# Attention and two feed-forward layers: the weight parts of the third product made beside the second

## The chip, the cores and the metric

The kernel runs on one core of one Trainium2 chip. The metric is the time of one execution on the device in microseconds (us). The kernel before was timed in 3 runs; the median is 1670.05 us.

## The reference

The inputs are q, k, v (batch 8, 8 heads, 576 positions, head size 64) and four weight matrices, all float32. First comes softmax attention inside chunks of 64 positions; its output is laid out as 4608 tokens with 512 features. Then two feed-forward layers follow, each with an inner size of 2048:

```
x = attention(q, k, v)                            # 4608 x 512
x = square(relu(x @ moe_w_in)) @ moe_w_out        # products 1 and 2
h = x @ moe2_w_in                                 # product 3
g = where(h >= 1, h, where(h <= -1, 0, (h + 1)**2 / 4))
out = g @ moe2_w_out                              # product 4
```

The weights come as float64 and are read as pairs of 32-bit words; the kernel decodes them to float32 on the chip.

## The kernel before

**Arithmetic.** Every float32 product is made of three matmuls on parts: an operand is split into hi (rounded) and lo (what is left), and hi x hi, lo x hi and hi x lo are added up. Products 2 to 4 are done in seven block products (P1 to P7) instead of eight, by a scheme of sums of blocks (Strassen and Winograd). So from four blocks of a weight, four sums are made, and the seven block operands that are used are each split into hi and lo.

**Stages.** Four stages follow each other on TensorE (PE). The first makes product 1 block by block of 512 tokens, with the attention of the following tokens beside it. The second (w = 0 in the code) makes product 2, the third product 3, the fourth (w = 1) product 4. Results go through DRAM from stage to stage.

**Order.** The order of the work is written out by hand. Time is counted in slots: one slot is 6 matmuls of a product on PE. `pe_slot` puts matmuls into a slot, `at_slot` the work of the other engines and the DMAs. The program is emitted slot by slot, and each engine works through its own queue strictly in this order, waiting on semaphores. All DMAs are issued by SyncE's queue (SP), so one DMA that waits holds up every later one.

**The first stage** has 288 slots. The attention is done in 72 units of four heads and 128 tokens; from the twelfth on, one unit's turn stands in every four slots (`turn`, PER = 4). A turn loads q and k of the unit four turns on, and every second turn the v of a token tile (`load_v`, 4 DMAs, in slot 4k + 3), which the product with the attention weights (`att_d`, line 367) uses three turns later, in slot 4k + 12. The squares of each product-1 tile are written by GpSimd (line 425) and stored to DRAM (line 431). Besides, 48 weight units are made, one in 5.1 slots: m = 0 for w_out1 (product 2), m = 1 for w_in2 (product 3), m = 2 for w_out2 (product 4), 16 of each. Every unit is loaded by two DMAs (`stage_unit`) and decoded on ACT and DVE (`unit_a`, the first line of `unit_b`). For m = 0 and m = 1 GpSimd then makes the four sums (`sums`, line 184), ACT casts seven blocks to hi (`unit_c`, line 209), DVE subtracts to lo (`unit_d`, line 218), and SP stores hi and lo, 448 KB each (lines 213 and 219). For m = 2 only the four decoded blocks are stored (`wq`, 256 KB, line 201). From slot 192 to 238 SP also loads the first 24 weight tiles of product 2 (`load_w`, line 245). Units of m = 1 stand in slots 103 to 185, those of m = 2 from slot 185 on.

**The second stage** has 280 slots: five pairs of token ranges, each with seven ranks of eight slots, one for each block product. For each two slots `prep_b` puts a split of one operand on ACT (line 443, cast to oh) and DVE (line 444, subtraction to ol) into the program, five slots ahead, into one of three buffer pairs; `comb_b` makes the sums of raw operands on DVE (line 448). `load_g` (line 547) loads the raw operands of the next pair. GpSimd has nothing to do there.

**The third stage** also makes what is left of m = 2: `late_a` loads the four blocks of a unit, `late_b` makes the sums on GpSimd, `late_c` the cast on ACT (line 233), `late_d` the subtraction on GpSimd (line 238) and both stores, at 0, 4, 6 and 7 slots from the unit's start, one unit in ten slots. These four steps share one tile for the blocks and one for hi. The r tiles 10, 11 and 12 (`rt`) hold squares in the first stage and activations in the third; the second stage does not use them.

Of the kernel before, what the change touches and what calls it, by code (L numbers as in the profile page):

```python
# [8 lines left out]
F32 = mybir.dt.float32  # L9
F32R = mybir.dt.float32r  # L10
U32 = mybir.dt.uint32
AF = mybir.ActivationFunctionType
ALU = mybir.AluOpType
AX = mybir.AxisListType

P = 128
# [7 lines left out]

FMAX = 3.4028234663852886e38
RANK = ("P1", "P5", "P6", "P3", "P7", "P2", "P4")
CIDX = {"P4": 0, "P1": 1, "P2": 2, "P5": 3, "P6": 4, "P7": 5, "P3": 6}
SIZES = (448, 448, 448, 480, 480)


# [1 line left out]
def chunk_attention_moe_moe2(ctx, tc, q, k, v, w_in1, w_out1, w_in2, w_out2, out):  # L32
# [10 lines left out]
    nc = tc.nc  # L43
# [9 lines left out]
    HF = NF // 2  # L53
# [10 lines left out]
    mp = ctx.enter_context(tc.tile_pool(name="mp", bufs=1))  # L64
    dram = ctx.enter_context(tc.tile_pool(name="dram", bufs=1, space=bass.MemoryType.DRAM))
# [4 lines left out]
    def f(ap):  # L70
        return ap.bitcast(F32)
# [8 lines left out]
        return pool.tile(shape, dt, tag=f"q{tag}", name=name, padded_shape=[P, 2, n])  # L80

    def rt(tag, shape, name, dt=F32, padded=None):
        return mp.tile(shape, dt, tag=f"r{tag}", name=name, padded_shape=padded or [P, 512])

    def bank(i, shape, name, padded=None):
        return ps.tile(shape, F32, tag=f"b{i}", name=name, padded_shape=padded or [P, 512])
# [10 lines left out]

    wd = {(m, a): dram.tile([P, 2, 2, 7, P], F32, name=f"w{m}_{a}") for m in range(3) for a in range(8)}

    wq = {(a, b): dram.tile([P, 4, P], F32, name=f"q{a}_{b}") for a in range(8) for b in range(2)}  # L100

# [2 lines left out]
    wst = {}  # L106
# [51 lines left out]
    def stage_unit(m, a, b):  # L158
        t = ep.tile([P, 4 * P, 2], U32, tag="ws", name="wu", bufs=2)
        w = (w_out1, w_in2, w_out2)[m]  # L160
        if m == 1:
            src = w.rearrange("(kh kt p) f -> kt p kh f", kh=2, kt=2)[b]
            cols = [(a + fh * HF) * 2 * P for fh in (1, 0)]
        else:
            src = w.rearrange("(kh kk p) d -> kk p kh d", kh=2, kk=HF)[a]
            cols = [(2 * dh + b) * 2 * P for dh in (1, 0)]
        for i, c in enumerate(cols):
            nc.sync.dma_start(
                out=t[:, 2 * i * P:2 * (i + 1) * P].rearrange("p (h f) w -> p h (f w)", h=2),
                in_=src[:, :, c:c + 2 * P],  # L170
            )
        wst[m, a, b] = t
# [7 lines left out]

    def sums(c):

        for o, x, z, op in ((4, 0, 1, ALU.add), (6, 2, 0, ALU.subtract), (5, 4, 2, ALU.subtract), (7, 3, 5, ALU.subtract)):
            nc.gpsimd.tensor_tensor(out=c[:, o], in0=c[:, x], in1=c[:, z], op=op)

    def store_parts(m, a, b, hi, lo):
        nc.sync.dma_start(out=wd[m, a][:, 0, b], in_=f(hi))
        nc.sync.dma_start(out=wd[m, a][:, 1, b], in_=f(lo))

    def unit_b(m, a, b):  # L190
        y, ab = wst[m, a, b]
        if m == 2:
            c = ep.tile([P, 4, P], F32, tag="wl", name="wq", bufs=2, padded_shape=[P, 7, P])
        else:
            c = ep.tile([P, 8, P], F32, tag="wc", name="wc", bufs=1)
        nc.vector.scalar_tensor_tensor(
            out=c[:, 0:4].rearrange("p a f -> p (a f)"), in0=ab, scalar=TINY, in1=f(y), op0=ALU.is_ge, op1=ALU.mult
        )
        wst[m, a, b] = c
        if m == 2:  # L200
            nc.sync.dma_start(out=wq[a, b], in_=c[:, 0:4])
            del wst[m, a, b]
        else:
            sums(c)

    def unit_c(*u):
        c = wst[u]
        hi = ep.tile([P, 7, P], F32R, tag="wh", name="wh", bufs=2)
        nc.scalar.copy(hi, c[:, 1:8])
        wst[u] = (c, hi)  # L210

    def unit_hi(m, a, b):
# [2 lines left out]
    def unit_d(m, a, b):  # L215
        c, hi = wst.pop((m, a, b))
        lo = ep.tile([P, 7, P], F32R, tag="wl", name="wl", bufs=2)
        nc.vector.tensor_tensor(out=lo, in0=c[:, 1:8], in1=f(hi), op=ALU.subtract)
        nc.sync.dma_start(out=wd[m, a][:, 1, b], in_=f(lo))


    def late_a(a, b):
        c = mp.tile([P, 8, P], F32, tag=f"q{LATE[0]}", name="lc")
        nc.sync.dma_start(out=c[:, 0:4], in_=wq[a, b])
        wst[a, b] = c

    def late_b(a, b):
        sums(wst[a, b])

    def late_c(a, b):  # L230
        c = wst[a, b]
        hi = mp.tile([P, 7, P], F32R, tag=f"q{LATE[1]}", name="lh", padded_shape=[P, 8, P])
        nc.scalar.copy(hi, c[:, 1:8])
        wst[a, b] = (c, hi)

    def late_d(a, b):
        c, hi = wst.pop((a, b))
        nc.gpsimd.tensor_tensor(out=c[:, 1:8], in0=c[:, 1:8], in1=f(hi), op=ALU.subtract)
        store_parts(2, a, b, hi, c[:, 1:8])

    wt = {}

# [383 lines left out]
    SB1 = 2 * NF * NBL  # L626
# [9 lines left out]
    LATE = (4, 5)  # L636
# [9 lines left out]
    def at_slot(s, fn, *args):  # L646
        s = int(s)
        assert cur[0] is None or s >= cur[0], (s, cur)
        todo.setdefault(s, []).append((fn, args))
# [4 lines left out]
    with tc.manual_schedule():  # L654
        early = tc.tile_pool(name="early", bufs=1, side="right")
        ep = early.__enter__()
# [93 lines left out]
        for n, u in enumerate(units):  # L750
            g = U0 + n * UPER
            if n < 2:
                at_slot(g - 3 + n, stage_unit, *u)
            at_slot(g, unit_a, *u)
            if n + 2 < len(units):
                at_slot(g, stage_unit, *units[n + 2])
            at_slot(g + 2, unit_b, *u)
            if u[0] < 2:
                at_slot(g + 4, unit_c, *u)
                at_slot(g + 5, unit_hi, *u)  # L760
                at_slot(g + 6, unit_d, *u)
# [44 lines left out]
        for kp in range(4):  # L806
            for n, i in enumerate((0, 1, 3)):
                at_slot(done + 1 + 5 * n + kp, load_g, 0, 0, i, kp)
            at_slot(SB1 + 4, load_g, 0, 0, 2, kp)

        for j in range(NPAIR):
            for i in range(HF):
                b = SA2 + 7 * (HF * j + i)
                for prod, o in OFFS.items():
                    pe_slot(b + o, form_a, j, i, prod)
        for j in range(NPAIR):
            if j == 0:
                e = SA2
                loads = tuple(e - 24 + n for n in range(4))
                times = dict(P1=e - 14, P5=e - 11, P6=e - 8, P3=e - 6, P2=e - 3, P7=e - 2, P4=e + 1)  # L820
            else:
                b = SA2 + 7 * (HF * j - 1)
                l0 = SA2 + 7 * (HF * (j - 1) + 2)
                loads = tuple(l0 + 7 * n for n in (0, 1, 3, 2))
                times = dict(P1=b - 8, P5=b, P6=b + 4, P3=b + 3, P2=b + 5, P7=b + 10, P4=b + 10.5)
            for i in range(4):
                at_slot(loads[i], load_xa, j, i, A_RAW[i])
            for prod in sorted(ORD, key=times.get):
                at_slot(times[prod], prep_a, j, prod)
                if prod in AFTER:  # L830
                    at_slot(times[prod] + (4 if prod == "P2" and j else 1), comb_a, j, prod)
            if j + 1 < NPAIR:
                for n in range(4):
                    g = SA2 + 56 * j + 12 + 10 * n
                    u = divmod(4 * j + n, 2)
                    for d, fn in ((0, late_a), (4, late_b), (6, late_c), (7, late_d)):
                        at_slot(g + d, fn, *u)


        for t in range(56):  # L840
# [63 lines left out]
```

## Time and profile before

| what | us |
|---|---|
| median of 3 runs (1668.27 to 1672.38) | 1670.05 |
| the profiled execution | 1671.81 |
| its span, first to last instruction | 1670.0 |
| first stage ends | 593.5 |
| second stage | 593.5 to 946.6 |
| third stage | 946.6 to 1307.8 |
| fourth stage | 1307.8 to 1662.5 |
| PE / DVE / ACT / GpSimd busy in the span | 1613.6 / 1140.2 / 891.8 / 420.3 |

All times inside the profile are microseconds from the first instruction. Busy time of an engine doesn't count DMA issue, so SP's work is read from its own rows in order of time. A row of waits names the instruction that waited and the one that released it. Loads of matmul weights into PE (PEld) run beside matmuls. PE's granted clock is 0.993 of full speed over the span.

### The profile page before, as it was taken

Reading aid. Unit: us, or ns where it says so; the run is one execution under the profiler, and the core shown is the slowest. Engines: PE = TensorE matmul, PEld = TensorE weight load, DVE = VectorE, ACT = ScalarE, POOL = GpSimd, SP = SyncE. Lnnn points to the kernel's source line nnn. Section 1 sums busy time; section 2 is a strip of 40 time slices with the busy share of each in tenths; the row PEclk is TensorE's granted clock in tenths of the full one; section 3 lists DMA queues with packets and bytes.
Section 4 is the critical chain, followed back from the end, with each engine's and each line's share of the span. In section 5 each row is a group of like instructions: output and inputs, shape, how many; then the busy total and the mean of one; then the engine's idle time right before and its main releaser. Section 6 shows DMA issues by size and latency. Waiting matters only on the chain.

```text
span 1670.0 us, 27722 instructions
## 1 busy us (share of the span) xinstructions
PE 1613.6 (97%) x9504; PEld 1384.6 (83%) x9504; DVE 1140.2 (68%) x1576; ACT 891.8 (53%) x1852; POOL 420.3 (25%) x466
## 2 busy tenths in 40 slices
PE   6889999999999999999999999999999999999998
PEld 4667777777777889999888898988888899998887
DVE  6967666666645267677677757667574778777776
ACT  6656666666555244444444566666665544444442
POOL 2546565556433410000000234344240000000000
PEclk9999999999999999999999999999999999999999
DMA  7667888888888897335277864655659963654723
GB/s 186 185 183 227 266 267 275 263 271 276 254 254 262 265 290 237 98 123 174 72 230 208 247 229 162 240 173 181 227 201 340 306 188 82 161 140 103 200 40 48
DMA packets 445645, 339.51 MB, mean 203 GB/s; under 512 B 217152, under 2 KB 421952, under 8 KB 445504
## 3 DMA queue, kind: packets, MB, share of 16 engines
q1 hardware_dynamic: 445504, 337.74, 67.2%
q8 instruction: 75, 1.23, 0.3%
q14 instruction: 66, 0.54, 0.1%
HBM read 195.04 MB, written 142.61 MB: 202 GB/s over the span
## 4 chain that ended last, share of the span: by engine, by line
PE 79%; DVE 7%; DMA 7%; issue 3%; ACT 2%; POOL 1%; SPq 1%; POOLq 0%; DVEq 0%; ACTq 0%
PE X L454 31%; PE ph L412 19%; PE V L454 17%; PE W L454 7%; DMA vt<-in_v_dram 2%; PE psD L367 2%; DMA wu<-in_moe_w_out_dram 1%; PE psB L311 1%; PE psA L294 1%; DVE wy L115 1%; DMA ws<-in_moe_w_in_dram 1%; DVE ol L444 1%; DVE wy L118 1%; PE psC L352 1%; DVE t L535 1%
## 5 line engine op out<-in xcount | busy, mean ns | idle before, releaser
L454 PE MATMUL X<-oh,w 128*128 128x448 f32 (+1 forms) x1920 | 557.8, 371 | 5.1 <-DVE c L515 5.0
L443 ACT CAST oh<-gr 128x896 fp32r<-128x896 f32 (+1 forms) x280 | 270.0, 964 | 335.0 <-PE X L454 158.1
L444 DVE TENSOR_TENSOR ol<-gr,oh 128x896 fp32r<-128x896 f32 (+1 forms) x280 | 314.4, 1124 | 182.1 <-ACT oh L443 173.4
L454 PEld LDWEIGHTS X<-oh,w 128*128 128x128 f32 x1920 | 360.0, 188 | 48.2 <-ACT t L529 4.3
L454 PE MATMUL X<-ol,w 128*128 128x448 f32 (+1 forms) x960 | 356.7, 372 | 6.4 <-POOL ol L444 5.2
L454 PE MATMUL V<-oh,w 128*128 128x448 f32 (+1 forms) x960 | 278.5, 371 | 0.0
L412 PE MATMUL ph<-xh,ih 128*128 128x512 f32 x576 | 246.5, 428 | 0.2 <-ACT g L424 0.2
L412 PE MATMUL ph<-xl,ih 128*128 128x512 f32 x576 | 228.9, 397 | 0.0
L412 PE MATMUL ph<-xh,il 128*128 128x512 f32 x576 | 228.8, 397 | 0.0
L425 POOL TENSOR_TENSOR g<-g 128x512 f32<-128x512 f32 x144 | 169.6, 1178 | 158.2 <-ACT g L424 148.8
L454 PEld LDWEIGHTS X<-ol,w 128*128 128x128 f32 x960 | 180.1, 188 | 29.7 <-POOL ol L444 6.8
L454 PEld LDWEIGHTS V<-oh,w 128*128 128x128 f32 x960 | 180.2, 188 | 20.9
L448 DVE TENSOR_TENSOR gr<-gr,gr 128x896 f32<-128x896 f32 (+1 forms) x160 | 177.8, 1111 | 3.6 <-DMA gr<-g 3.6
L454 PE MATMUL V<-ol,w 128*128 128x448 f32 (+1 forms) x480 | 178.0, 371 | 0.0
L424 ACT ACTIVATE g<-ph 128x512 f32<-128x512 f32 x144 | 86.5, 601 | 110.7 <-PE ph L412 100.5
L454 PE MATMUL W<-oh,w 128*128 128x448 f32 (+1 forms) x480 | 139.4, 371 | 0.0
L412 PEld LDWEIGHTS ph<-xl,ih 128*128 128x128 f32 x576 | 109.9, 191 | 25.0
L412 PEld LDWEIGHTS ph<-xh,ih 128*128 128x128 f32 x576 | 109.9, 191 | 22.3 <-ACT g L424 0.5
L444 POOL TENSOR_TENSOR ol<-xr,oh 128x896 fp32r<-128x896 f32 (+1 forms) x15 | 36.5, 2434 | 363.2 <-ACT oh L443 352.1
L412 PEld LDWEIGHTS ph<-xh,il 128*128 128x128 f32 x576 | 110.6, 192 | 16.9
L529 ACT ACTIVATE t<-c,half 128x448 f32<-128x448 f32 (+1 forms) x120 | 81.2, 681 | 71.2 <-DVE c L515 71.0
L535 DVE SCALAR_TENSOR_TENSOR t<-c,t 128x448 f32<-128x448 f32 (+1 forms) x120 | 93.1, 802 | 17.6 <-ACT t L529 17.4
(69 smaller groups left out, 2014.2 us busy)
## 6 DMA issues: line engine op xcount, KB each, us to landing
w<-w SPq DMA_DIRECT2D x168, 256.0 KB, 5.2
gr<-g SPq DMA_DIRECT2D x96, 448.0 KB, 5.1
gr<-g SPq DMA_DIRECT2D x64, 480.0 KB, 4.6
g<-t SPq DMA_DIRECT2D x96, 224.0 KB, 2.6
wu<-in_moe_w_out_dram SPq DMA_DIRECT2D x64, 256.0 KB, 4.8
g<-t SPq DMA_DIRECT2D x64, 240.0 KB, 5.0
w<-wh SPq DMA_DIRECT2D x32, 448.0 KB, 3.8
w<-wl SPq DMA_DIRECT2D x32, 448.0 KB, 4.7
```

The source lines that it names most:

```text
L115: nc.vector.scalar_tensor_tensor(out=y, in0=w1, scalar=0xC0000000, in1=y, op0=ALU.bitwise_and, op1=ALU.bitwise_or)
L118: nc.vector.scalar_tensor_tensor(out=y, in0=w0, scalar=29, in1=y, op0=ALU.logical_shift_right, op1=ALU.bitwise_or)
L367: nc.tensor.matmul(pt[rows(e), e, p * P + c * CH:p * P + (c + 1) * CH], vt[u // UT % NV][rows(e), c, u % UT * NP + p, :], at[rows(e), p, r ...
L412: nc.tensor.matmul(ph, win[fi][wi][:, kt * P:(kt + 1) * P], x[:, i, :], start=(kt == 0 and a == 0), stop=(kt == KT - 1 and a == 2),)
L424: nc.scalar.activation(out=g, in_=ph, func=AF.Relu)
L425: nc.gpsimd.tensor_tensor(out=g, in0=g, in1=g, op=ALU.mult)
L443: nc.scalar.copy(hi, raw)
L444: eng.tensor_tensor(out=lo, in0=raw, in1=f(hi), op=ALU.subtract)
L448: eng.tensor_tensor(out=o, in0=x, in1=z, op=ALU.subtract)
L454: nc.tensor.matmul(o, wt_[:, wi, c, :], x[:, i, :], start=first and a == 0, stop=last and a == 2, skip_group_check=True,)
L529: nc.scalar.activation(out=t, in_=h, func=AF.Square, bias=half, scale=0.5)
L535: nc.vector.scalar_tensor_tensor(out=t, in0=h, scalar=1.0, in1=t, op0=ALU.max, op1=ALU.min)
```

## The change

The units of m = 1 get the treatment that those of m = 2 have. In the first stage they are only decoded, and their four blocks are stored in DRAM (`wq`, now also keyed by m). Sums, hi and lo are made in the second stage by the same four `late` steps, in halves of a unit (64 of 128 columns): 32 halves, one in 7.5 slots, from slot 2 of the second stage to slot 241. A half loads 128 KB in pieces of 256 bytes; its two stores write 224 KB each in pieces of 256 bytes. Its tiles are r10 and r12 in turn for the blocks and r11 for hi. The 32 halves are finished before the weights of product 3 are loaded from slot 224 of the stage on, unit by unit.

A unit's tile holds seven blocks instead of eight: one sum is written over a block that no later sum reads, the block pairs are loaded in the other order, and the table CIDX that finds a block product's weights follows. In the third stage the units of m = 2 stay whole and where they were.

```diff
--- before.py
+++ after.py
@@ -24,7 +24,7 @@
 
 FMAX = 3.4028234663852886e38
 RANK = ("P1", "P5", "P6", "P3", "P7", "P2", "P4")
-CIDX = {"P4": 0, "P1": 1, "P2": 2, "P5": 3, "P6": 4, "P7": 5, "P3": 6}
+CIDX = {"P1": 0, "P2": 1, "P7": 2, "P4": 3, "P5": 4, "P6": 5, "P3": 6}
 SIZES = (448, 448, 448, 480, 480)
 
 
@@ -80,7 +80,9 @@
         return pool.tile(shape, dt, tag=f"q{tag}", name=name, padded_shape=[P, 2, n])
 
     def rt(tag, shape, name, dt=F32, padded=None):
-        return mp.tile(shape, dt, tag=f"r{tag}", name=name, padded_shape=padded or [P, 512])
+        if padded is None:
+            padded = [P, 512] if len(shape) == 2 else [P, shape[1], 512 // shape[1]]
+        return mp.tile(shape, dt, tag=f"r{tag}", name=name, padded_shape=padded)
 
     def bank(i, shape, name, padded=None):
         return ps.tile(shape, F32, tag=f"b{i}", name=name, padded_shape=padded or [P, 512])
@@ -97,7 +99,7 @@
 
     wd = {(m, a): dram.tile([P, 2, 2, 7, P], F32, name=f"w{m}_{a}") for m in range(3) for a in range(8)}
 
-    wq = {(a, b): dram.tile([P, 4, P], F32, name=f"q{a}_{b}") for a in range(8) for b in range(2)}
+    wq = {(m, a, b): dram.tile([P, 4, P], F32, name=f"q{m}_{a}_{b}") for m in (1, 2) for a in range(8) for b in range(2)}
 
 
 
@@ -160,10 +162,10 @@
         w = (w_out1, w_in2, w_out2)[m]
         if m == 1:
             src = w.rearrange("(kh kt p) f -> kt p kh f", kh=2, kt=2)[b]
-            cols = [(a + fh * HF) * 2 * P for fh in (1, 0)]
+            cols = [(a + fh * HF) * 2 * P for fh in (0, 1)]
         else:
             src = w.rearrange("(kh kk p) d -> kk p kh d", kh=2, kk=HF)[a]
-            cols = [(2 * dh + b) * 2 * P for dh in (1, 0)]
+            cols = [(2 * dh + b) * 2 * P for dh in (0, 1)]
         for i, c in enumerate(cols):
             nc.sync.dma_start(
                 out=t[:, 2 * i * P:2 * (i + 1) * P].rearrange("p (h f) w -> p h (f w)", h=2),
@@ -180,25 +182,21 @@
 
     def sums(c):
 
-        for o, x, z, op in ((4, 0, 1, ALU.add), (6, 2, 0, ALU.subtract), (5, 4, 2, ALU.subtract), (7, 3, 5, ALU.subtract)):
+        for o, x, z, op in ((4, 2, 3, ALU.add), (2, 0, 2, ALU.subtract), (5, 4, 0, ALU.subtract), (6, 1, 5, ALU.subtract)):
             nc.gpsimd.tensor_tensor(out=c[:, o], in0=c[:, x], in1=c[:, z], op=op)
-
-    def store_parts(m, a, b, hi, lo):
-        nc.sync.dma_start(out=wd[m, a][:, 0, b], in_=f(hi))
-        nc.sync.dma_start(out=wd[m, a][:, 1, b], in_=f(lo))
 
     def unit_b(m, a, b):
         y, ab = wst[m, a, b]
-        if m == 2:
+        if m > 0:
             c = ep.tile([P, 4, P], F32, tag="wl", name="wq", bufs=2, padded_shape=[P, 7, P])
         else:
-            c = ep.tile([P, 8, P], F32, tag="wc", name="wc", bufs=1)
+            c = ep.tile([P, 7, P], F32, tag="wc", name="wc", bufs=1)
         nc.vector.scalar_tensor_tensor(
             out=c[:, 0:4].rearrange("p a f -> p (a f)"), in0=ab, scalar=TINY, in1=f(y), op0=ALU.is_ge, op1=ALU.mult
         )
         wst[m, a, b] = c
-        if m == 2:
-            nc.sync.dma_start(out=wq[a, b], in_=c[:, 0:4])
+        if m > 0:
+            nc.sync.dma_start(out=wq[m, a, b], in_=c[:, 0:4])
             del wst[m, a, b]
         else:
             sums(c)
@@ -206,7 +204,7 @@
     def unit_c(*u):
         c = wst[u]
         hi = ep.tile([P, 7, P], F32R, tag="wh", name="wh", bufs=2)
-        nc.scalar.copy(hi, c[:, 1:8])
+        nc.scalar.copy(hi, c)
         wst[u] = (c, hi)
 
     def unit_hi(m, a, b):
@@ -215,28 +213,40 @@
     def unit_d(m, a, b):
         c, hi = wst.pop((m, a, b))
         lo = ep.tile([P, 7, P], F32R, tag="wl", name="wl", bufs=2)
-        nc.vector.tensor_tensor(out=lo, in0=c[:, 1:8], in1=f(hi), op=ALU.subtract)
+        nc.vector.tensor_tensor(out=lo, in0=c, in1=f(hi), op=ALU.subtract)
         nc.sync.dma_start(out=wd[m, a][:, 1, b], in_=f(lo))
 
 
-    def late_a(a, b):
-        c = mp.tile([P, 8, P], F32, tag=f"q{LATE[0]}", name="lc")
-        nc.sync.dma_start(out=c[:, 0:4], in_=wq[a, b])
-        wst[a, b] = c
-
-    def late_b(a, b):
-        sums(wst[a, b])
-
-    def late_c(a, b):
-        c = wst[a, b]
-        hi = mp.tile([P, 7, P], F32R, tag=f"q{LATE[1]}", name="lh", padded_shape=[P, 8, P])
-        nc.scalar.copy(hi, c[:, 1:8])
-        wst[a, b] = (c, hi)
-
-    def late_d(a, b):
-        c, hi = wst.pop((a, b))
-        nc.gpsimd.tensor_tensor(out=c[:, 1:8], in0=c[:, 1:8], in1=f(hi), op=ALU.subtract)
-        store_parts(2, a, b, hi, c[:, 1:8])
+    n_l = [0]
+
+    def late_a(m, a, b, h):
+        n_l[0] += 1
+        cols = slice(0, P) if m == 2 else slice(h * P // 2, (h + 1) * P // 2)
+        if m == 2:
+            c = mp.tile([P, 7, P], F32, tag=f"q{LATE[0]}", name="lc", padded_shape=[P, 8, P])
+        else:
+            c = rt(10 + 2 * (n_l[0] % 2), [P, 7, P // 2], "lc")
+        nc.sync.dma_start(out=c[:, 0:4], in_=wq[m, a, b][:, :, cols])
+        wst[m, a, b, h] = c, cols
+
+    def late_b(*u):
+        sums(wst[u][0])
+
+    def late_c(*u):
+        c, cols = wst[u]
+        if u[0] == 2:
+            hi = mp.tile([P, 7, P], F32R, tag=f"q{LATE[1]}", name="lh", padded_shape=[P, 8, P])
+        else:
+            hi = rt(11, [P, 7, P // 2], "lh", F32R)
+        nc.scalar.copy(hi, c)
+        wst[u] = (c, cols, hi)
+
+    def late_d(*u):
+        c, cols, hi = wst.pop(u)
+        nc.gpsimd.tensor_tensor(out=c, in0=c, in1=f(hi), op=ALU.subtract)
+        m, a, b, h = u
+        nc.sync.dma_start(out=wd[m, a][:, 0, b, :, cols], in_=f(hi))
+        nc.sync.dma_start(out=wd[m, a][:, 1, b, :, cols], in_=c)
 
     wt = {}
 
@@ -755,7 +765,7 @@
             if n + 2 < len(units):
                 at_slot(g, stage_unit, *units[n + 2])
             at_slot(g + 2, unit_b, *u)
-            if u[0] < 2:
+            if u[0] == 0:
                 at_slot(g + 4, unit_c, *u)
                 at_slot(g + 5, unit_hi, *u)
                 at_slot(g + 6, unit_d, *u)
@@ -807,6 +817,11 @@
             for n, i in enumerate((0, 1, 3)):
                 at_slot(done + 1 + 5 * n + kp, load_g, 0, 0, i, kp)
             at_slot(SB1 + 4, load_g, 0, 0, 2, kp)
+
+        for n in range(32):
+            u = (1, n // 4, n // 2 % 2, n % 2)
+            for d, fn in ((0, late_a), (4, late_b), (6, late_c), (7, late_d)):
+                at_slot(SB1 + 2 + 7.5 * n + d, fn, *u)
 
         for j in range(NPAIR):
             for i in range(HF):
@@ -834,7 +849,7 @@
                     g = SA2 + 56 * j + 12 + 10 * n
                     u = divmod(4 * j + n, 2)
                     for d, fn in ((0, late_a), (4, late_b), (6, late_c), (7, late_d)):
-                        at_slot(g + d, fn, *u)
+                        at_slot(g + d, fn, 2, *u, 0)
 
 
         for t in range(56):
```

## Rows read from the trace of the kernel before

**Rows 1.** busy us (count): PE, PEld, DVE, ACT, POOL; clock, DMA, GB/s
```profile
258.40:414.40 156.00, 151.88 (x1281) 120.73 (x1279) 105.90 (x200) 101.53 (x315) 92.93 (x125) 0.98 0.87 268
414.40:565.00 150.60, 144.59 (x1103) 115.14 (x1100) 80.27 (x165) 78.46 (x254) 60.95 (x61) 1.00 0.87 256
...
593.50:946.60 353.10, 352.22 (x1681) 315.08 (x1681) 258.95 (x254) 156.90 (x183) 6.82 (x4) 1.00 0.60 182
```

**Rows 2.** what PE waited for, 258.4 to 565: total us, times, longest
```profile
PE psD L367 <- DMA vt<-in_v_dram: 7.6, 9, 2.5
PE psD L367 <- ACT wa L111: 1.5, 1, 1.5
```

**Rows 3.** chain that ended last: start, us, what
```profile
349.36 2.95 PE ph L412 x12
356.60 2.95 PE ph L412 x12
```

**Rows 4.** by stretch, of line 412 alone: PE busy (count), PEld busy (count)
```profile
46.10:318.20 272.10, 217.77 (x811) 148.63 (x811) 0.97 0.79 237
...
258.37:412.03 153.66, 127.92 (x481) 87.52 (x481) 0.98 0.87 268
412.03:530.10 118.07, 94.11 (x361) 64.26 (x362) 1.00 0.88 257
```

**Rows 5.** SP's queue in order of time, 330 to 344: start, us, what
```profile
329.63 0.42 SPq L431 DMA_DIRECT2D g<-g  x1
330.14 0.40 SPq L213 DMA_DIRECT2D w<-wh  x1
330.65 1.56 SPq L168 DMA_DIRECT2D wu<-in_moe_w_in_dram  x2
332.30 0.99 SPq L431 DMA_DIRECT2D g<-g  x2
333.41 3.29 SPq L283 DMA_DIRECT2D vt<-in_v_dram  x4
```

**Rows 6.** PE in order of time, 338 to 340 [idle before <- releaser]
```profile
339.09 1.05 PE L367 MATMUL psD<-atT,vt 64*64 64x64 f32 x12 [2.48 <-DMA vt<-in_v_dram]
```

**Rows 7.** instructions of the tiles wl and wq: ns min/median/max, first and last start
```profile
L218 DVE TENSOR_TENSOR wl<-wc,wh x32: 1075/1092/1931, 122.8 to 420.2; 128x896 fp32r<-128x896 f32 x32
L219 SPq DMA_DIRECT2D w<-wl x32: 338/457/1136, 124.0 to 429.8; - x32
...
  DVE wq L196: 5.8, 2
...
L201 SPq DMA_DIRECT2D q<-wq x16: 364/402/1124, 433.2 to 563.8; - x16
```

**Rows 8.** what SP's queue waited for, 258.4 to 414.4
```profile
SPq L431 <- POOL wc L184: 3.8, 9, 0.8
```

**Rows 9.** DVE in order of time, 660 to 675
```profile
668.29 1.09 DVE L444 TENSOR_TENSOR ol<-gr,oh 128x896 fp32r<-128x896 f32 x1 [0.26 <-ACT oh L443]
```

**Rows 10.** PE in order of time, 668 to 673
```profile
672.59 0.37 PE L454 MATMUL V<-ol,w 128*128 128x448 f32 x1
```

**Rows 11.** by tile: qkn (258 to 565), lc, gr and w (593 to 946)
```profile
DMA to landing us min/median/max: 2.3/3.0/4.2
...
L184 POOL TENSOR_TENSOR lc<-lc x64: 452/462/932, 963.3 to 1220.6; 128x128 f32<-128x128 f32 x64
...
L233 ACT CAST lh<-lc x16: 927/944/947, 968.2 to 1221.5; 128x896 fp32r<-128x896 f32 x16
L238 POOL TENSOR_TENSOR lc<-lc,lh x16: 2127/2134/2335, 969.2 to 1222.5; 128x896 f32<-128x896 f32 x16
...
DMA to landing us min/median/max: 3.4/5.1/7.0
...
L245 SPq DMA_DIRECT2D w<-w x78: 517/571/1787, 596.6 to 944.7; - x78
```

**Rows 12.** what ACT waited for, 946 to 1308
```profile
ACT lh L233 <- POOL lc L184: 3.5, 4, 1.6
```

## Prediction

> **What bounds the kernel now.** I read the stages first, as stretches of time: the first product with the attention beside it ends at 593.5 us, the second product (w = 0) runs to 946.6, the third to 1307.8, the fourth to the end. In the second product TensorE is busy 352.22 of 353.10 us, GpSimd 6.82 and DVE 258.95 [rows 1]: that stage has no time to give, only time to lose. In the two stretches of the first stage in which the units of w_in2 (m = 1, 258.4 to 414.4) and of w_out2 (m = 2, 414.4 to 565.0) are made, TensorE is short of its stretch by 4.1 and 6.0 us, and the DMA engines stand at 0.87 [rows 1].
>
> Next, what TensorE waits for there: the load of v, 7.6 us in 9 waits of 10.1 in all; nothing else is above 1.5 [rows 2]. TensorE's own beat says how much is lost with all that follows a wait: an undisturbed turn (four slots, 24 matmuls, and one attention unit) is 356.60 - 349.36 = 7.24 us [rows 3]. 480 matmuls (20 turns; one more is counted at the edge) took 153.66 us where 144.8 would do, so 8.9 us were lost; the next 360 (15 turns) took 118.07 instead of 108.6, 9.5 lost [rows 4]. That is 18.4 us in the stretch that the change touches.
>
> Then why v is late. SyncE's queue (SP) issues every DMA of the kernel, in program order. By 318.2 TensorE has started the 810 matmuls of slots 0 to 134 (and one more at the edge) [rows 4]. Slot 135 is where the program puts the load of the token tile that slot 144 uses. SP issues it at 333.41, 15.2 us after TensorE came to slot 135; TensorE stands 2.48 us and begins with that v at 339.09 [rows 5, 6]. SP does not idle before this: its rows follow each other with gaps of 0.09 to 0.12 us [rows 5]. So SP is a second full engine in this stage. It lags TensorE by two turns, and whenever the lag and the landing together pass the 16.3 us of the nine slots from 135 to 144 (9 x 7.24/4), TensorE pays.
>
> **The change part by part.**
> *First stage, taken out.* Each of 16 units of m = 1 loses its four sums on GpSimd, the cast on ACT, the subtraction on DVE, and the stores of hi and lo (448 KB each); it gets one store of the decoded blocks (256 KB). For SP that is one DMA less for a unit: 0.46 us of issue (the w<-wl median; the new store is like q<-wq, 0.40 [rows 7]) and 0.10 of gap, 16 x 0.56 = 9.0 us. SP also waited 3.8 us in this stretch for g behind GpSimd's sums [rows 8]; those sums go. SP's relief is thus 9.0 to 12.8 us. DVE, ACT and GpSimd each lose work too, but TensorE's waits there are for v, so I count that at nothing beyond the 3.8. The stalls of m = 1 go first; what SP has left over it carries into the stretch of m = 2, where 24 loads of w are squeezed in and the lag would otherwise build up again. As long as SP is the late queue, a microsecond that it saves is one that TensorE saves. Bounds for this step: 18.4 (no stall left) and 4 (what TensorE stands idle in the stretch of m = 1, with those of m = 2 as before). I take 10, a little over the issues alone. SP's lag at the loads of w is what is late next.
>
> *First stage, moved.* The border between units with hi and lo and units with a store of blocks comes 16 units earlier. The blocks' tile shares two buffers with lo, and DVE waited 5.8 us in two waits for the stores of lo at the old border [rows 7]. Behind it in DVE's queue stand the row maxima of the attention, on which the exponentials wait. At the old border TensorE shows no wait for DVE [rows 2]; at the new one SP lags about as much. Between 0 and 5.8 I take +0.5, near the old border's price on TensorE.
>
> *Second product, added.* 32 half units, one in 7.5 slots, which are 7.5 x 353.1/280 = 9.46 us: SP a load of 128 KB in 256-byte pieces and two stores of 224 KB in 256-byte pieces; GpSimd four sums of 64 columns and a subtraction of 448; ACT a cast of 448. What can reach TensorE:
> (a) ACT's queue. The cast waits for the sums, the sums for the load, and behind the cast stand the splits of the operands. The split of the second rank's first operand starts at 668.29, takes 1.09 and is first read at 672.59 [rows 9, 10]: 3.2 us ahead. So TensorE does not see an ACT delay up to some 3 us.
> (b) Whether that wait comes. Program order makes the half units serial: SP's store of n stands ahead of the load of n + 1. The loop is load 3.0 (the nearest row: q and k, up to 128 KB in 256-byte pieces) + four sums of 0.37 (between half of 0.462 and the whole) + cast 0.5 (half of 0.944, with a start) + subtraction 1.1 (half of 2.134) + issue of the second store 0.9 (over the 0.571 of w<-w in 512 pieces; here 896) + six semaphore steps of 0.1 = 7.6 us [rows 11]. That is under 9.46: ACT finds the sums ready. In the third product the same loop on whole units let ACT wait 3.5 us in all [rows 12]. At the far end (load 4.2, sums 0.93) it is 11.0, at the near end (2.3 and 0.23) 6.3.
> (c) SP itself: 96 issues of 0.6 to 0.9 us in 300. The raw loads for the next pair stand 11 slots and more ahead of their use, against a landing of 5.1 [rows 11].
> The first half unit's buffer holds one of the last g of the first stage, so SP holds the loads of w for some 3 us; these are wanted 30 slots later. For all this +1.0, between 0 and the price of rival 2.
>
> *Third product.* A unit's tile has seven blocks instead of eight, in another order; the same counts and sizes of operations: 0.
>
> Sum: -10 + 0.5 + 1.0 = -8.5. The profiled execution took 1671.8 us (span 1670.0), 1.8 over the median of the runs: 1663.3 by it, 1661.5 against the median of 1670.05.
>
> **The rivals.**
> 1. *SP's relief is used up* in the stretch of m = 2: the loads of w bring the lag back to its limit, and only m = 1's 4 us go. For it: 9.5 us are lost there although its units have three DMAs already. Against it: SP would start that stretch with less lag. -4 + 1.5 = -2.5: 1667.5.
> 2. *The loop in the second product outlasts its 7.5 slots* (slower than before). If the small loads land like gr (5.1) and the sums take 0.46, it is 5.1 + 1.84 + 0.5 + 1.1 + 0.9 + 0.6 = 10.0 us, 0.58 over; 32 x 0.58, less the cover of 3.2, is 15.4 us of TensorE, paid at the cast in ACT's queue. It outweighs the 9.5 of the first stage from a loop of 9.46 + 12.7/32 = 9.86. Net +5.9: 1676. For it: the DMA share of 0.60 goes up [rows 1]. Against it: q and k landed in 3.0 at a share of 0.87.
> 3. *GpSimd blocks DVE.* A subtraction of 896 columns on DVE took 1.08 at best and up to 1.93 in the first stage, where GpSimd works beside it [rows 7]. A half unit brings 2.6 us of GpSimd. Taken as a full block, DVE's demand in 303 us (240 slots) is 222 + 32 x 2.6 = 305: over the brim, and in the two ranks of each pair in which DVE both combines and evicts the cover of 3.2 goes. I price 0.8 us in each of these ten, 8 us: net -1.5, 1668.5. At half a block DVE has 264 of 303 and nothing is lost, which is what I take.
> The Trainium skill, SBUF — State Buffer (Who interferes with whom), says that a DVE instruction with two SBUF inputs contends with a GpSimd one that reads SBUF, and that whichever comes second waits for the whole of the other. By that rule rival 3 is the forecast. The spread from 1.075 to 1.931 agrees that they collide; the median of 1.092 doesn't show that most overlaps cost their whole length.
> 4. *All stalls go*: -18.4 + 1.5 = -16.9, 1653.
>
> **How the numbers follow.** Forecast 0.57 (own range 1657 to 1666), rival 1 0.18, rival 2 0.10, rival 3 0.10, rival 4 0.05. Less than 0.3% (5.0 us) can't be told from no change. Faster: 0.51 of the forecast, 0.04 of rival 1, 0.02 of rival 3, 0.05 of rival 4: 0.62. Same: 0.06 + 0.13 + 0.06 + 0.01 of rival 2 = 0.26. Slower: 0.09 of rival 2, 0.02 of rival 3, 0.01 of rival 1: 0.12. The range, 1654 to 1672, leaves out rival 2, most of rival 4 and the tails.
>
> **What would show it.** Right: the lag of SP behind slot 135 falls under 12 us, TensorE's waits for v shrink below 5 us, the first stage ends near 584, the second product lasts 353 to 355. Wrong: v is late by the same amount with SP idle before it (then the transfer, not the queue, is the limit); ACT's lh waits for lc by more than 20 us in the second product, with TensorE waiting for ol (rival 2); DVE's splits there at 1.4 and over with TensorE waiting (rival 3).

## Result: slower by 1%, and the profile after

The changed kernel takes 1686.74 us (median of 4 runs, 1684.11 to 1688.01); the kernel before took 1670.76 beside it. The ratio is 1.0095, 95% interval 1.0076 to 1.0113. Forecast were 1661.5 and a range up to 1672: the first stage gained about what was forecast, and the second lost twice as much.

| stage (us of the profiled run) | before | after | |
|---|---|---|---|
| first stage ends | 593.5 | 580.3 | -13.2 |
| second stage | 353.1 | 380.2 | +27.1 |
| third stage | 361.2 | 362.6 | +1.4 |
| fourth stage | 354.7 | 355.1 | +0.4 |
| span | 1670.0 | 1685.8 | +15.8 |

**First stage.** Matmuls of product 1 by stretch, slots 0 to 134, 104 to 183 and 184 to 243 (PE busy with count, PEld busy with count, clock, DMA share, GB/s); the counterparts are [rows 4]:

```profile
45.60:314.90 269.30, 217.45 (x811) 148.69 (x811) 0.97 0.78 234
...
255.40:403.50 148.10, 126.91 (x480) 86.74 (x481) 0.99 0.79 230
403.50:517.00 113.50, 94.97 (x360) 64.89 (x361) 0.98 0.82 238
```

480 matmuls take 148.10 us, 3.3 above the undisturbed 144.8; the next 360 take 113.50, 4.9 above 108.6. So 8.2 us are lost where 18.4 were. This profile and those of eight runs below have the same first stage; they lose 4.5 to 8.2 us in these slots and end the stage between 577.4 and 583.1 us. So the gain there is 10 to 14 us, and a difference of some 4 us between two such profiles shows nothing by itself. TensorE comes to slot 135 at 314.9 and SP issues that slot's load of v 9.2 us later, against 15.2 [rows 4, 5]. Here is SP's queue around it (start, us, what), and then the only group of TensorE's waits from 255 to 552 (total, times, longest):

```profile
320.40 0.51 SPq L199 DMA_DIRECT2D q<-wq  x1
321.00 0.88 SPq L441 DMA_DIRECT2D g<-g  x2
321.98 0.95 SPq L170 DMA_DIRECT2D wu<-in_moe_w_in_dram  x2
323.03 0.95 SPq L441 DMA_DIRECT2D g<-g  x2
324.07 1.98 SPq L293 DMA_DIRECT2D vt<-in_v_dram  x3
```

```profile
PE psD L377 <- DMA vt<-in_v_dram: 4.0, 3, 2.6
```

Three waits for v are left of nine [rows 2], and at the loads of w SP is late again: its lag at slot 223 is back at 16.6 us, and most of the 4.9 us that TensorE still loses stand near slot 232, where the longest wait of 2.6 us is.

**Second stage.** By stretch (busy us with count of PE, PEld, DVE, ACT, POOL; clock, DMA share, GB/s), to be read against the last of [rows 1]:

```profile
580.30:960.50 380.20, 364.11 (x1681) 317.83 (x1680) 266.89 (x254) 167.34 (x215) 122.29 (x164) 0.98 0.78 219
```

TensorE stands idle 16.1 us of this stage where it was 0.9; that is 15.2 of the 27.1. The other 11.9 are matmuls that last longer (364.11 us busy against 352.22 for the same count). A part of these is the clock: behind the three longest stalls (3.4, 1.5 and 1.4 us) the granted clock fell to 0.50, the lower level of 1.2 GHz, for 13.7 us in all; in the kernel before it did not fall in this stage. Three of these microseconds (us, PE busy with count, clock, DMA share, GB/s):

```profile
813.00:816.00 3.00, 2.80 (x7) 0.50 0.82 229
```

At half the clock 13.7 us do the work of 6.9, so about 6.9 of the 11.9 are the clock (an estimate from these numbers). So these stalls cost more than their own length.

What ACT waited for in it, then TensorE, then SP (lc is a half unit's tile of blocks and sums, later lo; lh its tile of hi; gr, oh and ol are raw operands and their hi and lo; X, V and W are the banks of results):

```profile
ACT lh L241 <- POOL lc L186: 113.9, 28, 8.6
ACT oh L453 <- PE X L464: 38.6, 26, 3.5
```

```profile
PE X L464 <- ACT oh L453: 6.5, 5, 3.4
PE X L464 <- DVE ol L454: 4.7, 8, 0.9
PE W L464 <- ACT oh L453: 1.9, 2, 1.4
```

```profile
SPq L248 <- ACT lh L241: 80.7, 21, 7.2
SPq L557 <- DVE gr L458: 39.2, 25, 3.9
SPq L249 <- POOL lc L246: 16.9, 21, 1.0
```

ACT's cast waits 28 times out of 32 for the sums, 113.9 us; in the kernel before, ACT waited for little else than TensorE in this stage. The third fence is the one that explains: SP stands 80.7 us at the store of hi, that is, it waits for the very cast that is late, and the next half unit's load stands behind that store. One such round in order of time, first SP, then GpSimd, ACT and TensorE:

```profile
802.77 2.54 SPq L229 DMA_DIRECT2D lc<-q  x1
805.40 1.50 SPq L557 DMA_DIRECT2D gr<-g  x1
810.23 0.37 SPq L248 DMA_DIRECT2D w<-lh  x1
811.44 0.37 SPq L249 DMA_DIRECT2D w<-lc  x1
811.90 1.01 SPq L606 DMA_DIRECT2D y<-c  x2
813.01 0.53 SPq L229 DMA_DIRECT2D lc<-q  x1
```

```profile
808.23 1.36 POOL L186 TENSOR_TENSOR lc<-lc 128x64 f32<-128x64 f32 x4 [8.67 <-DMA lc<-q]
810.28 1.14 POOL L246 TENSOR_TENSOR lc<-lc,lh 128x448 f32<-128x448 f32 x1 [0.69 <-ACT lh L241]
```

```profile
809.62 0.57 ACT L241 CAST lh<-lc 128x448 fp32r<-128x448 f32 x1 [5.93 <-POOL lc L186]
810.10 0.96 ACT L602 COPY c<-X 128x448 f32<-128x448 f32 x2
810.95 2.79 ACT L453 CAST oh<-gr 128x960 fp32r<-128x960 f32 x3
```

```profile
812.01 0.69 PE L464 MATMUL X<-oh,w 128*128 128x480 f32 x2 [1.51 <-ACT oh L453]
```

The load goes out at 802.77 and its data are there at 808.2. ACT has stood since 803.7 (5.93 us), with evictions and three operand casts behind it; the cover of 3 us is used up, TensorE stands 1.51, and the clock falls as shown above. SP can't move between 806.9 and 810.23. Its next load goes out at 813.01, late again. The prices of this loop (ns min/median/max, first and last start; from 580 to 912):

```profile
L186 POOL TENSOR_TENSOR lc<-lc x128: 293/324/1909, 587.8 to 911.8; 128x64 f32<-128x64 f32 x128
L229 SPq DMA_DIRECT2D lc<-q x32: 523/598/4171, 585.1 to 907.1; - x32
L246 POOL TENSOR_TENSOR lc<-lc,lh x31: 1140/1167/1782, 592.2 to 905.5; 128x448 f32<-128x448 f32 x31
...
DMA to landing us min/median/max: 2.5/3.5/7.5
```

(The row of landings counts the stores from lc too; the 32 loads alone landed in 3.5 us in the median.) Load follows load by (907.1 - 585.1)/31 = 10.4 us, where 7.5 slots of the old length are 9.46.

### The profile page after: what moved, and what is told of

Its sections match the earlier page's. It is cut to its first block, busy times and chain, and to the rows that moved or that the text cites. A ratio compares the mean times of both kernels' runs of the same rounds, so it can differ in the third digit from the quotient of the medians.

```text
span 1685.8 us, 28003 instructions
## 1 busy us (share of the span) xinstructions
PE 1620.3 (96%) x9504; PEld 1383.3 (82%) x9504; DVE 1126.9 (67%) x1560; ACT 888.9 (53%) x1868; POOL 504.1 (30%) x562
## 5 line engine op out<-in xcount | busy, mean ns | idle before, releaser
L454 DVE TENSOR_TENSOR ol<-gr,oh 128x896 fp32r<-128x896 f32 (+1 forms) x280 | 319.1, 1145 | 201.2 <-ACT oh L453 200.7
L464 PEld LDWEIGHTS X<-oh,w 128*128 128x128 f32 x1920 | 362.6, 189 | 56.8 <-ACT oh L453 8.5
L453 ACT CAST oh<-gr 128x896 fp32r<-128x896 f32 (+1 forms) x280 | 266.6, 964 | 250.5 <-PE X L464 115.5
L464 PE MATMUL X<-ol,w 128*128 128x448 f32 (+1 forms) x960 | 360.1, 375 | 10.4 <-POOL ol L454 5.2
L186 POOL TENSOR_TENSOR lc<-lc 128x64 f32<-128x64 f32 (+1 forms) x192 | 107.9, 572 | 322.3 <-DMA lc<-q 314.8
L458 DVE TENSOR_TENSOR gr<-gr,gr 128x896 f32<-128x896 f32 (+1 forms) x160 | 183.6, 1147 | 3.8 <-DMA gr<-g 3.8
```

What stands on the lines that cost most here:

```text
L453: nc.scalar.copy(hi, raw)
L454: eng.tensor_tensor(out=lo, in0=raw, in1=f(hi), op=ALU.subtract)
L458: eng.tensor_tensor(out=o, in0=x, in1=z, op=ALU.subtract)
L464: nc.tensor.matmul(o, wt_[:, wi, c, :], x[:, i, :], start=first and a == 0, stop=last and a == 2, skip_group_check=True,)
```

## Experiments

Theory A: loads, sums, cast and stores of the half units are one chain through SP's and ACT's queues with too little time from load to cast. Theory B: GpSimd's work blocks DVE. Theory C: SP and the DMA engines are overloaded by small pieces. All edits are to the changed kernel, unless another is named. The lengths, from the profile of each run; the time is the median of 4 to 9 executions for after, ahead, ahead24, spread and swap24, and a single execution for the other edits, so for those the lengths of the stages are the evidence and a microsecond or two between them is not:

| run | first stage ends | second stage | ACT's wait for lc | time |
|---|---|---|---|---|
| before | 593.5 | 353.1 | - | 1670.8 |
| after | 580.3 | 380.2 | 113.9 | 1686.7 |
| wide | 580.0 | 371.5 | 99.7 | 1675.0 |
| wide_lead | 580.9 | 364.3 | 62.6 | 1668.3 |
| swap | 580.0 | 360.8 | 36.1 | 1662.5 |
| late24 | 582.9 | 368.6 | 98.4 | 1674.4 |
| poolcast | 577.4 | 367.5 | none | 1674.3 |
| ahead | 578.6 | 357.1 | 13.2 | 1663.2 |
| ahead24 | 581.9 | 355.1 | 9.3 | 1662.5 |
| spread | 577.0 | 355.7 | 4.1 | 1661.6 |
| swap24 | 578.3 | 354.3 | 12.7 | 1657.7 |
| less_pool | 583.1 | 355.6 | 5.3 | 1663.2 |
| whole_load | 582.4 | 378.7 | 108.8 | 1689.1 |
| more_bytes | 601.2 | 379.1 | 121.7 | 1702.6 |

**ahead** and **ahead24**: sums, cast and stores four slots later, so that the next load goes out first; in the second also a later start.

```diff
-            for d, fn in ((0, late_a), (4, late_b), (6, late_c), (7, late_d)):
-                at_slot(SB1 + 2 + 7.5 * n + d, fn, *u)
+            for d, fn in ((0, late_a), (8, late_b), (10, late_c), (11, late_d)):
+                at_slot(SB1 + 2 + 7.5 * n + d, fn, *u)     # ahead24: SB1 + 24
```

> The load of each half unit stays where it is; sums, cast and subtraction come four slots later (8, 10, 11 instead of 4, 6, 7), so that the load of half n+1 now stands ahead of the stores of half n in SyncE's queue. Amount of work, pieces and queues are the same. Theory A (the half units form one serial loop through SyncE's queue that is longer than its 7.5 slots, and ACT's cast waits in front of the operands' splits): ACT's wait of lh for lc falls from 114 us to under 30, the second stage from 380 to 354 to 362 us, the whole to 1658 to 1668. Theory B (GpSimd's work blocks DVE and makes the splits late): the second stage stays at 370 or more. Theory C (SyncE and the DMA engines are overloaded by 256-byte pieces): it stays at 370 or more, with SyncE late throughout.

> As the run with the load ahead, and the first half unit starts in slot 24 of the second stage instead of slot 2, behind the burst of 24 weight loads. Theory A with the burst as a cause of its own (in the changed kernel 11 us of the 26 lost stand in slots 35 to 46, after SyncE fell 13 us behind): the second stage 353 to 357, 2 to 5 us under the run that starts in slot 2, the whole about 1658 to 1661. Theory B: 370 or more, as there. If the burst costs nothing, the two runs are within 1 us.

23.1 and 25.1 of the 27.1 us of the second stage go, with the same work, pieces and queues. Both beat the kernel before: ratios 0.9945 (0.9926 to 0.9965) and 0.9948 (0.9930 to 0.9965). Theory A holds; B and C don't. In ahead, 3.7 us are still lost in slots 39 to 41, and none there in ahead24, so the burst of weight loads is a cause of its own, though the times of the two runs don't separate. What ACT's cast waits for just ahead of that stall is not the sums but the one tile for hi, that is, the store of the half before. In ahead, and then in swap (below), whose two stalls in the burst come behind the same wait; from 615 to 645:

```profile
ACT lh L241 <- DMA w<-lh: 6.3, 1, 6.3
```

```profile
ACT lh L241 <- DMA w<-lh: 14.5, 2, 7.6
```

The column of the table above leaves this wait out; over the whole stage it is 16.0 us in ahead and 17.3 in swap, and none in after. In ahead24 the half units look like this (580 to 937):

```profile
L186 POOL TENSOR_TENSOR lc<-lc x128: 290/1032/1271, 621.1 to 913.0; 128x64 f32<-128x64 f32 x128
...
DMA to landing us min/median/max: 2.4/4.2/7.8
```

Loads land later (3.9 us for the loads alone, against 3.5) and the median sum takes three times as long as in the changed kernel. Neither price is felt as long as the cast comes late enough.

**wide**: `8.4 * n` for `7.5 * n`. **wide_lead**: besides, `(7.4, late_c), (8.3, late_d)`.

> The changed kernel with one half unit in 8.4 slots instead of 7.5, the order of the queues as it was. Theory A: the loop of about 10 us fits into 8.4 x 1.26 = 10.6 us, so what is lost in the second stage falls from 27 us to 10 to 16, most of it in the burst at the start. Theory B: the same work of GpSimd against the same work of DVE in 260 instead of 232 slots, so 27 falls by a tenth or so, to 22 to 26.

> One half unit in 8.4 slots, as in the wide run, and the cast and the stores 1.4 slots later; the load still stands behind the stores of the half before in SyncE's queue. It gives the load the same extra time before its cast as the run with the load 1.5 slots earlier, without the change of order. If the order is the cause (the load waits for the stores of the half before, and these for the late cast), the second stage stays within 4 us of the wide run's 371.5, at 367 or more. If the time between load and cast is the cause, it comes down to about 360, as with the load 1.5 slots earlier.

A slower rate alone leaves 18.4 of 27.1 us, where the loop had given 10 to 16. Of the 18.4, 5.6 are lost in the burst and 5.6 in the slots 270 to 279, where the last half units now run into the preparation of the third stage. All runs whose half units end behind slot 260 lose 1.0 to 5.6 us in those ten slots; after, swap, ahead and whole_load lose nothing there. The other 12.8 are what the loop had given, though less than half of them lie in the burst, where most were expected. With 1.4 slots more between load and cast, and the order of the queue kept, 7.2 more go and ACT's wait falls from 99.7 to 62.6; what is left is 5.9 in the burst (slots 39 to 42) and 5.5 at 275 to 277, the end of the stage again. So more time helps without a change of the order. Which share the order has is not settled, for 364.3 lies between the two expectations.

**swap**: `(-1.5, late_a)` for `(0, late_a)`. **late24**: `SB1 + 24` for `SB1 + 2`.

> The changed kernel with only the load of each half unit 1.5 slots earlier, just enough to stand ahead of the stores of the half before in SyncE's queue; sums, cast and stores stay. Theory A, with the queue's order as the cause: the load no longer waits for the subtraction and the stores (1.2 + 2 us of the loop), ACT's wait falls from 114 to 20 to 50 us, the second stage from 380 to 358 to 365. If it is only the time between load and cast that counts, 1.5 slots (1.9 us) of it take away 32 x 1.9 us at most of ACT's wait but the order nothing: 365 to 372. Theory B (GpSimd blocks DVE): no change, 375 or more.

> The changed kernel with the first half unit in slot 24 instead of slot 2 and the order as it was. What the burst of weight loads costs by itself: the stalls of slots 35 to 46 (11 us) go and the second stage takes 366 to 372; if the same stalls come at another place, it stays at 377 or more. Theory B: 378 to 382.

1.5 slots of lead, with the load now ahead of the stores, give back 19.4 us; outside the burst only 1.1 at slot 278 is left, as in the kernel before. Starting behind the burst gives back 11.6 by itself, as expected.

**poolcast**: the half units' cast on GpSimd.

```diff
-        nc.scalar.copy(hi, c)
+        if u[0] == 2:
+            nc.scalar.copy(hi, c)
+        else:
+            nc.gpsimd.tensor_copy(out=hi, in_=c)
```

> The changed kernel with the cast to hi of the half units on GpSimd instead of ACT. ACT then waits for nothing of the half units. Theory A (the price is paid at ACT's queue): the second stage comes down to 353 to 358 although GpSimd gets more work and the loop is longer. Theory B: GpSimd works more beside DVE, so the second stage stays at 380 or grows, with DVE's splits late. Theory C: it stays near 380.

About half of the loss goes (12.7 us), not all: a miss for the strict form of A. What SP and ACT wait for here:

```profile
SPq L251 <- POOL lh L244: 112.0, 30, 8.5
...
ACT oh L456 <- DMA gr<-g: 21.9, 7, 6.0
```

SP still stands at the store, and the raw operands' loads behind it come late; over half of what is left, 8.2 us, is lost in slots 271 to 274. So a late half unit reaches TensorE by two queues, ACT's and SP's.

**less_pool**: ahead24 without `nc.gpsimd.tensor_tensor` in `late_d` for m = 1.

> The version with the load ahead and the start in slot 24; it leaves out the half units' subtraction on GpSimd, so the blocks themselves stand where lo should. About half of GpSimd's work in the second stage is gone. Theory B would make the 2.0 us that this version still loses in the second stage (355.1 against 353.1) go down to about 1; theory A alone leaves it at 354 to 356. In either case the subtractions and sums of DVE there come down from 1.13 and 1.25 us (896 columns) towards 1.10 and 1.08.

The run leaves out the half units' subtraction. Second stage 355.6, as with it (355.1). B's share in TensorE's time is nothing measurable, though DVE's splits of 896 do come down from 1.13 to 1.11 us and its sums from 1.25 to 1.12.

**whole_load**: blocks of a half side by side, two stores for a unit, load pieces of 1 KB.

```diff
-            nc.sync.dma_start(out=wq[m, a, b], in_=c[:, 0:4])
+            if m == 2:
+                nc.sync.dma_start(out=wq[m, a, b], in_=c[:, 0:4])
+            else:
+                for h in range(2):
+                    nc.sync.dma_start(out=wq[m, a, b][:, h], in_=c[:, 0:4, h * P // 2:(h + 1) * P // 2])
... (the shape of wq and the load in late_a follow)
```

> The changed kernel with the blocks of each half unit side by side in DRAM: a unit's blocks are stored by two DMAs of 128 KB in the first stage, and a half unit's load has 1 KB pieces instead of 256 bytes. Second stage: if the small pieces of the load make the loop long, landing falls from 3.9 to about 3 us and the stage by 10 to 20 us (32 x 0.9, less what is hidden); if SyncE's order is the cause, by 5 or less. First stage: SyncE now issues four DMAs for a unit of m = 1, as many as before the change, while sums, cast and subtraction stay away. If the gain of 13 us comes from SyncE's issues, the stage ends at 586 to 592; if it comes from GpSimd, ACT and DVE, at 579 to 582.

**more_bytes**: a second store of 640 KB for a unit of m = 1.

```diff
             nc.sync.dma_start(out=wq[m, a, b], in_=c[:, 0:4])
+            if m == 1:
+                nc.sync.dma_start(out=wx[a, b], in_=c[:, 0:2].unsqueeze(1).to_broadcast([P, 5, 2, P]))
... (wx is a new DRAM tensor that nobody reads)
```

> The changed kernel with a second store for each unit of m = 1 in the first stage: 640 KB of copies of two blocks into DRAM that nobody reads. So SyncE has four DMAs for such a unit and the engines move 896 KB of stores, as before the change, while sums, cast and subtraction stay away. With four DMAs of fewer bytes the stretch lost 8.6 us (slots 104 to 244), with the old work 18.4. If the bytes made the difference (fuller DMA engines, longer issues, later landings), the lag of SyncE goes back to 12 to 15 us at the slots 135 to 183, and 14 to 18 us are lost, the stage ending at 587 to 592. If it was the work on GpSimd, ACT and DVE, 8 to 10 us are lost and the stage ends at 580 to 584. The second stage stays as in the changed kernel, 378 to 382.

The two narrow down where the first stage's gain comes from. Product 1's matmuls by the same two stretches, whole_load and then more_bytes:

```profile
257.30:406.30 149.00, 125.38 (x480) 85.57 (x480) 1.00 0.81 221
406.30:519.10 112.80, 95.06 (x360) 65.00 (x360) 0.98 0.87 247
```

```profile
256.30:417.30 161.00, 129.35 (x481) 88.37 (x481) 0.97 0.85 257
417.30:537.40 120.10, 96.44 (x360) 65.98 (x361) 0.97 0.86 249
```

With four DMAs a unit, as before the change, 4.2 + 4.2 = 8.4 us are lost: the gain stays, at the low end of its spread. With the old number of bytes too (256 and 640 KB against twice 448), 16.2 + 11.5 = 27.7 are lost, though sums, cast and subtraction are away: the gain is gone, and more (14 to 18 were expected). So the number of issues is not the cause, and more bytes are enough to undo the gain. That the engines' work has no share in it is not shown: no run kept that work without its bytes. (The number did move SP's lag at slot 135, from 9.2 to 12.6 us in whole_load, but not as far as TensorE feels it.) SP feels the bytes: its 230 issues between the v loads of the slots 103 and 183 take 0.55 us each in whole_load and 0.63 in more_bytes (0.585 for 228 in the kernel before). The 80 stores of squares among them are the same in both and take 0.52 us each and then 0.68. In more_bytes SP's lag at slot 135 is 17.3 us. That more_bytes loses more than the kernel before is in part the clock: it is granted at 0.50 for 17.1 us of these slots, against 6.8 us in the kernel before. The rest is open; the copies are 1 KB pieces where hi and lo had 3.5.

In whole_load the second stage takes 378.7 us, 1.5 less than in after; in more_bytes, whose second stage is that of after, it took 379.1. So no gain of larger pieces is shown: C falls for that part.

**spread**: ahead24, with the 24 weight loads of the first stage at every third slot from 168. **swap24**: swap and spread, with the half units' loads from slot 24.5.

```diff
-            s = 2 * NF * (NBL - 3) + 2 * t if t < 24 ...
+            s = 2 * NF * (NBL - 3) - 24 + 3 * t if t < 24 ...
```

> The version with the load ahead and the start in slot 24, and the 24 weight loads of the first stage spread: from slot 168 every third slot instead of from slot 192 every second. By the lag of SyncE (5 us at slot 183, 16 at slot 231) the stall of about 4 us near slot 232 goes: the first stage ends 3 to 5 us earlier, near 577, and the whole takes 1657 to 1660. If that stall isn't SyncE's lag, no change: 1662.

> Three edits together: the load 1.5 slots earlier, the first half unit behind the burst of weight loads (loads from slot 24.5), and the 24 weight loads of the first stage spread as before. If the two causes add up (the order 19 us, the burst what is left of 8 us), the second stage takes 353 to 356, the first ends near 577, the whole takes 1657 to 1662, the same as with the load 4 slots ahead. If the short lead is not enough, ACT waits over 15 us for lc and the second stage takes 358 or more.

In spread 3.2 us are lost in the slots 104 to 243 and in swap24 1.6, both under the 4.5 to 8.2 of the nine profiles with the changed kernel's first stage. The first stage ends at 577.0 and 578.3, which is in their spread or next to it, and spread's time, 1661.6, doesn't separate from ahead24's. swap24 has the lowest median, 1657.7 us, ratio to before 0.9913 (0.9880 to 0.9946); the interval overlaps with those of ahead, ahead24 and spread. Its second stage:

```profile
578.30:932.60 354.30, 352.61 (x1681) 314.88 (x1680) 277.42 (x254) 172.45 (x215) 151.49 (x164) 1.00 0.82 233
```

TensorE is busy 352.61 us, as before the change (352.22 [rows 1]), with the whole added work in place.

## Why the prediction was wrong, step by step

- *What bounds the first stage.* Right: SP's lag and v. The size, 10 us, is what the slots 104 to 243 gave (18.4 - 8.2). The stage's other 3.0 lie before slot 104: TensorE came to that slot between 254.4 and 261.3 in runs that are equal up to there, so they are no gain. The term behind the 10 was wrong, and that it came out is luck: I counted one issue less for a unit, and whole_load, which has that issue back, loses no more than the spread of the others allows. Fewer bytes make the issues shorter (0.55 against 0.63 us, whole_load and more_bytes). v lands in 2.6 us in the median instead of 3.2, but the two runs don't trace that to the bytes (2.9 and 3.0).
- *The moved border.* 0.5 was forecast; TensorE shows no wait for DVE in the slots 104 to 243 of the changed kernel.
- *Second stage (b) is the step that failed*: "That is under 9.46: ACT finds the sums ready." ACT waited 113.9 us. The terms: sums 0.60 each in the mean (75.8 us in 128), not 0.37; landing 3.5 in the median and not 3.0; the load, which I let start on time, went out 7.0 us behind TensorE's slot in the mean, for SP stood behind stores and weight loads. I had taken a loop and compared its length with its spacing. The runs showed that the six slots between load and cast (6 x 353.1/280 = 7.6 us) decide: SP's delay, landing and sums had to fit into them, and they came to some 7.0 + 3.5 + 4 x 0.60 = 12.9; and a late cast made the next load later. The loop itself was mis-sized, too. Followed from load to load it took 10.4 us in the mean, not 7.6: landing 3.84, the four sums 2.53, cast 0.57, subtraction 1.24, the second store's issue 0.65, steps between engines 0.30, and 1.21 in which SP was still at other work ahead of that store or of the next load. That last term stood at nothing in the reckoning. Its far bound, 11.0, lay over 9.46, and yet the chance given to rival 2 was 0.10.
- *(a)*, the cover of 3 us, was right, if a little short: after none of ACT's waits for the sums up to 3.9 us did TensorE stand, and after each of 4.5 and more it did.
- *(c)*: SP by itself is no bound, but its order carried the delay on to the raw loads (poolcast).
- *Rival 2* named this place and this queue at a chance of 0.10, and its sign came (ACT's lh waited 113.9 us for lc, over 20). Its reckoning with the loop of 10.4 gives 32 x 0.94 - 3.2 = 27 us, and 27.1 was measured; but that is no test of it. The 10.4 comes from the slow run itself, and loads follow each other no faster than TensorE's slots, so a slow stage shows a long loop whatever slows it. Its own loop of 10.0 gave 15.4.
- *Rival 3* is out (less_pool, ahead24): the 8 us that I priced did not come. The rule of the Trainium skill (SBUF — State Buffer, Who interferes with whom), that whichever of the two comes second waits for the whole of the other, is no forecast of TensorE's time here. The collision itself agrees with it and is plain, mostly on GpSimd's side: 0.290 us at best and 1.032 in the median for one sum in ahead24.

## What to carry to other kernels

When work is added to an engine that is almost free, write down for each of its waits the time in the program between the transfer's issue and the first instruction that waits, and charge it with the issuing queue's own delay, not only with landing. A few slots of lead took no buffer beyond the two block tiles that were there, and were worth 19 to 25 us of the second stage (the 25 with a later start); larger pieces and less work on GpSimd showed no gain. A stall of TensorE can cost more than its length, because the clock may fall behind it. In a stage with a late DMA queue look at the bytes too, not only at the number of DMAs: here the gain stayed with the number back and was gone with the bytes back.

## What the runs showed of the hardware

A sum of 64 columns on GpSimd takes 0.29 us at best and a median of 1.03 in ahead24. There, the 90 sums that ran beside a subtraction or sum of DVE on raw operands took 1.10 in the median, and none of the 38 others over 0.34. DVE's own sums of 896 columns grow from 1.08 to 1.25 us in the mean (kernel before, ahead24), its subtractions from 1.10 to 1.13. The issue of a DMA on SP is not a fixed price: the same 128 KB load took from 0.52 to 4.17 us to issue in the changed kernel, and the same 80 stores 0.52 us each in the mean in whole_load and 0.68 in more_bytes.

After three stalls of TensorE (3.4, 1.5 and 1.4 us) in the second stage of the changed kernel, its granted clock stood at 0.50, 1.2 GHz, for 13.7 us in all; in the same stage of the kernel before, of ahead24 and of swap24, with waits of 0.9 to 2.6 us in all, it stayed at 1.00.
